# Fp32 pair loads, masks and conversions on GpSimd, and one score buffer given up for highway sums held in PSUM

## The chip, the cores and the metric

The kernel runs on one core of a Trainium2 chip. Times are microseconds (us) on the device for one execution of the whole program. A time that is quoted for a kernel is the median of several runs; comparisons use runs in the fast state only, with a 95% interval. The profile of each kernel is one execution, so the span that it shows is a little shorter than the timed run (134.9 us beside 136.6 us for the kernel before).

Engines: PE is TensorE (matmuls and transposes), DVE is VectorE, ACT is ScalarE, POOL is GpSimd, SP is SyncE, which here only issues DMA transfers.

## The reference

Windowed attention with sink tokens, then a highway layer. There are 4 batches, 8 heads, 768 tokens, head size 64; a token sees the 128 last tokens (itself included) and the first 4 of its batch.

```python
keep = is_sink | in_window          # (rel >= 0) & (rel < 128), or key position < 4
a = softmax(where(keep, q @ k.T / 8, -1e9))
x = (a @ v) -> (3072, 512)          # heads side by side
H = maximum(x @ w_h, 0);  T = sigmoid(x @ w_t + b_t)
out = T * H + (1 - T) * x           # 3072 x 512, fp32
```

Inputs are fp32: q, k and v are 18.9 MB together, the two weight matrices 2.1 MB. The kernel computes in fp16.

## The kernel before

A block is 128 tokens; there are 24 blocks, and c is the place of a block in its batch (0 to 5). For one block the work is: T (transpose q and k), S (scores against this block and the one before, and their exponentials), mask, A (attention times values, "av", and its division by the row sums, "xh"), X (transpose xh), Mt and Mh (the two highway matmuls, "tps" and "hps"), and three elementwise operations on VectorE: dd, ee and the output tokens otok. Blocks with c of 2 or more also need the scores of the four sink tokens ("sk").

The parts that matter here are the loads, the masks, the sink scores and the order of work:

```python
AHEAD = 8
s_ps  = tile_pool(name="ps_s",  bufs=2, PSUM)      # scores: two buffers of two banks
av_ps = tile_pool(name="ps_av", bufs=1, PSUM)
m_ps  = tile_pool(name="ps_m",  bufs=2, PSUM)      # everything else
def load(n):                      # the GpSimd queue converts fp32 -> fp16 on the way
    nc.gpsimd.dma_start(out=qsd, in_=q[b, :, rows, :].transpose([1, 0, 2]))
    nc.gpsimd.dma_start(out=ksd, in_=k[b, :, rows, :].transpose([1, 0, 2]))
# first loads: block 0, 1, q/k of 2, w_t, v of 2, q/k of 3, w_h, then v of 3, blocks 4, 5, ...
def stage_sink(n):
    for t in range(2):
        for hp in range(NHP):
            nc.tensor.matmul(sk[:, t, :], lhsT=ks[:, hp * P:(hp + 1) * P],
                             rhs=qT[:, hp, :], start=(hp == 0), stop=(hp == NHP - 1))
def stage_mask(n):
    for e in es:                  # two halves, 128 x 1024 each, on VectorE
        nc.vector.tensor_tensor(out=ev, in0=ev, in1=m..., op=ALU.mult)
def stage_Mh(n):
    ... hps = xT @ w_h ...
    dd   = max(hps, 0) - xh       # into SBUF, fp16
    ee   = (u + 1) * dd
    otok = 2 * xh + ee            # then stored
# ... (cuts)
for i in range(-2, NB + 1):
    s = i + 1
    if c(i) >= 2 and i % 2 == 0: stage_sink(i)
    stage_S(s)
    stage_A(i)
    stage_T(i + 2)                # the transposes of block i+2 stand BEHIND av of block i
    # loads of block i + 10
    stage_mask(s)
    stage_Mt(i - 1); stage_X(i); stage_Mh(i - 1)
```

TensorE, VectorE and ScalarE carry out their work in the order written, so a piece that waits holds back all that stands behind it on its engine.

The softmax here doesn't subtract the row's maximum and nothing guards it: scores larger than these inputs give would overflow.

## Time and profile before

| | before |
|---|---|
| median of 3 runs | 137.37 us (136.38 to 137.81) |
| span in the profile | 134.9 us |
| block 2 normalised (start of its xh on VectorE) | 26.80 us |
| mean distance of xh, blocks 2 to 19 | 4.70 us |
| mean distance of xh, blocks 19 to 23 | 4.63 us |
| xh of block 23 to the end | 9.75 us |

The last four rows split the span into a start, a steady part and a tail. They are read from the start times of the operation xh, once a block, in the time line of VectorE.

From the page of the kernel before: busy time of each engine; TensorE, VectorE and the DMA engines in 40 slices of the span (a digit is the busy share in tenths); two lines of the queues; and the chain of work that ended last, by engine.

```profile
PE 117.1 (87%) x1312; PEld 73.6 (55%) x1312; DVE 108.5 (80%) x230; ACT 90.4 (67%) x129; POOL 65.7 (49%) x81
...
PE   6657939999999899999999899999998999999720
...
DVE  6153724789988999899898998998989998999590
...
q0 software_dynamic: 75936, 10.49, 116.0%
...
HBM read 20.97 MB, written 6.29 MB: 202 GB/s over the span
...
DVE 33%; PE 32%; ACT 11%; issue 8%; POOL 7%; DMA 6%; DVEq 0%; POOLq 0%
```

TensorE and VectorE are full from slice 8 on, and they share the chain about equally. The busy times by stretch, 25 to 125 us in five stretches, sum to this (100 us in all):

```profile
sum 100.00, PE 96.58 PEld 62.16 DVE 91.97 ACT 77.72 POOL 45.54; mean PE 19.32 PEld 12.43 DVE 18.39 ACT 15.54 POOL 9.11
```

TensorE has 97 of 100 us here and VectorE 92. A converting load is counted by the fp16 bytes that it writes, which are half of what it reads.

VectorE's groups of instructions by line (busy us, mean ns of one | idle time before them and what ended it):

```profile
L247 DVE TENSOR_TENSOR e<-e,mask 128x1024 f16<-128x1024 f16 x32 | 20.5, 682 | 0.0
...
L313 DVE SCALAR_TENSOR_TENSOR dd<-hps,xh 128x512 f16<-128x512 f32 x24 | 16.5, 688 | 4.1 <-PE hps L310 4.1
```

The masks are 20.5 us in these 32 alone, two of 0.68 us a block, and dd waits 4.1 us in all for hps matmuls. The key copy (kT) takes 0.42 us. In the start, TensorE waits for block 3, in the time line of TensorE (start, us, ... , idle time before and what ended it):

```profile
19.49 0.40 PE L180 MATMUL tp<-ident,qsd 128*128 128x128 f16 x4 [1.93 <-DMA qsd<-in_q_dram]
20.32 0.61 PE L182 MATMUL tp<-ident,ksd 128*128 128x128 f16 x4 [0.43 <-DMA ksd<-in_k_dram]
```

### The profile page before, as it was taken

How to read it: one execution, taken by the hardware profiler on the slowest of the kernel's cores; microseconds unless marked ns; L12 is line 12 of the kernel's file. 1: busy time of each engine (PE TensorE's matmuls, PEld its weight loads, DVE VectorE, ACT ScalarE, POOL GpSimd, SP SyncE). 2: the span in 40 equal slices, each digit the busy share in tenths (PEclk: the TensorE clock that was granted, in tenths of full speed). 3: DMA queues.
4: the chain of work that ended last, by engine and by line, in shares of the span. 5: the costliest groups of instructions: out<-in, count | busy, mean ns of one | idle time of the engine just before them, and what ended most of it. 6: DMA issues, size and time to landing. Idle time of an engine off the chain costs nothing.

```text
span 134.9 us, 3378 instructions
## 1 busy us (share of the span) xinstructions
PE 117.1 (87%) x1312; PEld 73.6 (55%) x1312; DVE 108.5 (80%) x230; ACT 90.4 (67%) x129; POOL 65.7 (49%) x81
## 2 busy tenths in 40 slices
PE   6657939999999899999999899999998999999720
PEld 2225625856864466567565557656653685665300
DVE  6153724789988999899898998998989998999590
ACT  3054843779775977977777788779767977973310
POOL 6999747889897789979489370000000000000000
PEclk9999995999999999999999999999999999999996
DMA  0999999999999999999999999122011101101111
GB/s 4 111 123 127 160 188 160 155 181 171 154 198 191 196 151 148 152 195 240 192 194 179 193 194 176 38 80 80 6 78 78 63 19 78 78 5 78 78 78 78
DMA packets 81841, 17.02 MB, mean 126 GB/s; under 512 B 77729, under 2 KB 78753, under 8 KB 81826
## 3 DMA queue, kind: packets, MB, share of 16 engines
q0 software_dynamic: 75936, 10.49, 116.0%
q1 hardware_dynamic: 5890, 6.33, 14.6%
q8 instruction: 10, 0.16, 0.5%
q14 instruction: 5, 0.04, 0.1%
HBM read 20.97 MB, written 6.29 MB: 202 GB/s over the span
## 4 chain that ended last, share of the span: by engine, by line
DVE 33%; PE 32%; ACT 11%; issue 8%; POOL 7%; DMA 6%; DVEq 0%; POOLq 0%
PE hps L310 12%; ACT e L234 7%; DMA ksd<-in_k_dram 6%; DVE ee L316 6%; DVE otok L319 6%; DVE dd L313 6%; DVE e L247 5%; DVE xh L277 5%; PE tps L298 4%; PE xtp L286 4%; PE av L262 3%; DVE kT L186 3%; PE sk L211 3%; ACT qT L185 3%; POOL qsd L83 2%
## 5 line engine op out<-in xcount | busy, mean ns | idle before, releaser
L234 ACT ACTIVATE e<-sps,ebias 128x1024 f16<-128x1024 f32 (+1 forms) x48 | 47.4, 1039 | 11.2 <-PE sps L231 6.0
L298 PE MATMUL tps<-wt_sb,xT 128*128 128x512 f16 x96 | 25.5, 390 | 0.0
L310 PE MATMUL hps<-wh_sb,xT 128*128 128x512 f16 x96 | 24.7, 379 | 0.7
L83 POOL DMA_DIRECT2D qsd<-in_q_dram x24 | 21.6, 900 | 4.7 <-DMA wh_sb<-in_moe_w_h_dram 1.0
L84 POOL DMA_DIRECT2D ksd<-in_k_dram x24 | 21.4, 893 | 3.1 <-PE tp L182 1.3
L262 PEld LDWEIGHTS <-e 128*128 128x128 f16 x352 | 19.8, 98 | 3.2 <-issue 0.4
L301 ACT ACTIVATE u<-tps 128x512 f16<-128x512 f32 x24 | 14.4, 600 | 9.5 <-PE tps L298 9.5
L247 DVE TENSOR_TENSOR e<-e,mask 128x1024 f16<-128x1024 f16 x32 | 20.5, 682 | 0.0
L185 ACT COPY qT<-tp 128x512 f16<-128x512 f16 x24 | 14.0, 585 | 9.6 <-PE tp L182 9.6
L313 DVE SCALAR_TENSOR_TENSOR dd<-hps,xh 128x512 f16<-128x512 f32 x24 | 16.5, 688 | 4.1 <-PE hps L310 4.1
L186 DVE COPY kT<-tp 128x512 f16<-128x512 f16 x24 | 10.1, 423 | 11.7 <-ACT qT L185 11.7
L316 DVE SCALAR_TENSOR_TENSOR ee<-u,dd 128x512 f16<-128x512 f16 x24 | 16.6, 692 | 2.5
L319 DVE SCALAR_TENSOR_TENSOR otok<-xh,ee 128x512 f32<-128x512 f16 x24 | 16.6, 692 | 0.8
L277 DVE TENSOR_TENSOR xh<-av,rec 128x512 f16<-128x512 f32 x24 | 16.6, 691 | 0.8
L231 PE MATMUL sps<-qT,kT 64*128 64x128 f16 x352 | 15.4, 227 | 2.1 <-DVE kT L186 1.1
L231 PEld LDWEIGHTS <-kT 64*128 64x128 f16 x352 | 10.7, 98 | 9.5 <-issue 6.6
L288 ACT COPY xT<-xtp 128x512 f16<-128x512 f16 x24 | 14.0, 583 | 1.1 <-PE xtp L286 0.9
L298 PEld LDWEIGHTS <-xT 128*128 128x128 f16 x96 | 9.6, 100 | 9.1 <-issue 0.8
L310 PEld LDWEIGHTS <-xT 128*128 128x128 f16 x96 | 9.3, 98 | 8.6 <-issue 1.5
L286 PEld LDWEIGHTS <-xh 128*128 128x128 f16 x96 | 6.4, 101 | 13.4 <-DVE xh L277 11.2
L286 PE MATMUL xtp<-ident,xh 128*128 128x128 f16 x96 | 9.9, 228 | 3.8 <-DVE xh L277 3.8
L180 PE MATMUL tp<-ident,qsd 128*128 128x128 f16 x96 | 10.0, 231 | 2.4 <-DMA qsd<-in_q_dram 2.3
(88 smaller groups left out, 152.9 us busy)
## 6 DMA issues: line engine op xcount, KB each, us to landing
out_dram<-otok SPq DMA_DIRECT2D x24, 256.0 KB
qsd<-in_q_dram POOLq DMA_DIRECT2D x24, 128.0 KB, 7.3
ksd<-in_k_dram POOLq DMA_DIRECT2D x24, 128.0 KB, 7.4
wt_sb<-in_moe_w_t_dram POOLq DMA_DIRECT2D x1, 512.0 KB, 8.4
wh_sb<-in_moe_w_h_dram POOLq DMA_DIRECT2D x1, 512.0 KB, 10.1
v_91<-in_v_dram POOLq DMA_DIRECT2D x3, 128.0 KB, 8.0
v_92<-in_v_dram POOLq DMA_DIRECT2D x3, 128.0 KB, 6.1
v_93<-in_v_dram POOLq DMA_DIRECT2D x2, 128.0 KB, 8.0
```

The costliest lines, as they stand in the source:

```text
L83: nc.gpsimd.dma_start(out=qsd, in_=q[b, :, rows, :].transpose([1, 0, 2]))
L231: nc.tensor.matmul(sps[:, hh, o:o + P], lhsT=kk[rows, hp, :], rhs=qT[rows, hp, :], start=True, stop=True)
L234: nc.scalar.activation(out=e.rearrange("p a b c d -> p a (b c d)"), in_=sps[:, :, 0:2 * np_ * P], func=AF.Exp, bias=ebias, scale=SCALE)
L247: nc.vector.tensor_tensor(out=ev, in0=ev, in1=m.unsqueeze(1).to_broadcast([P, 4, np_ * P]), op=ALU.mult)
L262: nc.tensor.matmul(av[:, g, 2 * hl + hh, 0:_AVN], lhsT=es[g][:, hh, hl, pc, :], rhs=vt[:, 65 * h:65 * h + _AVN], start=first, stop=False, ...
L277: nc.vector.tensor_tensor(out=xh, in0=avh[:, :, 0:D], in1=rec.unsqueeze(2).to_broadcast([P, H, D]), op=ALU.mult)
L286: nc.tensor.transpose(xtp[:, j, :], xh[:, 2 * j:2 * j + 2, :], ident)
L298: nc.tensor.matmul(tps, lhsT=xT[:, kc, :], rhs=wt_sb[:, kc, :], start=False, stop=(kc == NOC - 1))
L310: nc.tensor.matmul(hps, lhsT=xT[:, kc, :], rhs=wh_sb[:, kc, :], start=(kc == 0), stop=(kc == NOC - 1))
L313: nc.vector.scalar_tensor_tensor(out=dd, in0=hps, scalar=0.0, in1=xh, op0=ALU.max, op1=ALU.subtract)
L316: nc.vector.scalar_tensor_tensor(out=ee, in0=u, scalar=1.0, in1=dd, op0=ALU.add, op1=ALU.mult)
L319: nc.vector.scalar_tensor_tensor(out=otok, in0=xh, scalar=2.0, in1=ee, op0=ALU.mult, op1=ALU.add)
```

## The change

Its intent: take the masks off VectorE. GpSimd spends its time issuing the converting loads, so these go first. After the first four blocks, q, k and v come as plain fp32 through SyncE's queue, two blocks at once for q and k (512 contiguous bytes rather than 256), and GpSimd converts them to fp16 in SBUF. GpSimd then has time for masks. The second score buffer (two PSUM banks) is given up so that the transposes, the bias, the sinks and the highway sum have banks of their own; the highway sum stays in PSUM through dd and ee, so that each of VectorE's large operations has only one SBUF input. The sink scores are made by narrow matmuls of 32 columns of weights each; the matmuls of their exponentials with the sinks' values (in av) use 64 rows of the array, and the bias row the other 64, so that these two can run side by side.

```diff
-    s_ps = ctx.enter_context(tc.tile_pool(name="ps_s", bufs=2, ...))
+    s_ps = ctx.enter_context(tc.tile_pool(name="ps_s", bufs=1, ...))
+    UB = 2; NFINE = 4; NV = 6
     def load_v(n):
-        nc.gpsimd.dma_start(out=vt[:, :, 0:D], in_=v[...])
+        nc.sync.dma_start(out=t, in_=v[...])                       # fp32
+    def load_unit(u):                                              # q, k of two blocks
+        nc.sync.dma_start(out=staged[name, u]...,
+            in_=src[b, :, t0:t0 + UW, :].rearrange("h (p j) d -> p h (j d)", j=UB))
+    def cast(name, u):  nc.gpsimd.tensor_copy(out=sd16[name, u]..., in_=staged...)
+    def cast_v(n):      nc.gpsimd.tensor_copy(...)
+    # first loads on GpSimd: block 0, 1, w_t, 2, w_h, 3
     def stage_T(n):
+        # tokens 2p+j of a pair lie in partition p: written back with stride two
+        dst = qkT_u[u].rearrange("p a (t j) -> p a t j", j=UB)[:, :, :, j]
     def stage_mask(n):
-        two products with a mask on VectorE
+        nc.gpsimd.affine_select(...)   # twice, 128 x 1024; chunks 0 and 1 partly on VectorE
     def stage_X(n):
-        nc.scalar.copy(out=xT, in_=xtp)
+        nc.vector.tensor_copy(out=xT, in_=xtp)
     def stage_Mh(n):
-        dd, ee in SBUF; otok in the same iteration
+        hps = max(hps, 0) - xh; hps = (u + 1) * hps      # in place, in PSUM
+    def stage_out(n): otok = 2 * xh + hps                # one iteration later
 # order of work
-    s = i + 1:  sink, S(s), A(i), T(i+2), mask, Mt(i-1), X(i), Mh(i-1)
+    s = i + 2
+    i == -2: load_unit(2), v 4, v 5, load_unit(3), v 6, v 7      # SyncE
+    S(s) first half, T(i+4), bias(i-1), A(i), out(i-2), S(s) second half, sink(i+1),
+    Mt(i-1), X(i), mask(s), Mh(i-1)
+    # T: i < 0: block i+3; i == 0: blocks 3 and 4; then block i+4
```

Note two things that are easy to pass over. The transposes now stand ahead of av in the order of TensorE, and they are those of block i+4. And scores of the first block of a pair need the transposes of both, because the pair's tokens are interleaved.

## The prediction

> **What bounds it now.** The span is 134.9 us. In the stretch view from 25 to 125 us, VectorE is busy 92 of 100 us, TensorE 97, ScalarE 78. The chain of waits gives VectorE 33% and TensorE 32%. One block takes about 4.65 us (first AV matmuls of block 2 at 25.3 us, of block 23 about 97 us later, 21 blocks). VectorE's work per block, from the group lines, is 4.6 us: two masks of 0.68, kT 0.42, xh, dd, ee, otok 0.69 each, rec 0.20. So VectorE is full and TensorE is nearly full. DMA is busy in every slice up to 84 us, but nothing waits for it after about 24 us: the loads bound the start only (k of block 3 lands at 20.3 us), not the steady part.
>
> **What the change does, per block.** VectorE loses the masks (kept for chunks 0 and 1, 0.68 each), gains xT (0.42, from ScalarE); kT is written with stride two and may go from 0.42 to 0.69. Sum about 4.1 us. ScalarE falls from about 4.0 to 3.4. TensorE saves the bias matmul (0.22) where it runs beside the sink matmuls, which use the other 64 rows: about 4.0.
> VectorE's remaining large operations have one SBUF input each, the other in PSUM. By the Trainium skill ("SBUF — State Buffer", Who interferes with whom) these do not contend with GpSimd; no trace shows it yet. GpSimd gets 1536 converted and up to 2048 masked elements a block. Its 128-element select took 0.33 us here; taking 0.1 us as fixed (its one-element memset) gives up to 1.8 ns an element. Estimate 3.5 to 5 us a block: below the period if lucky.
>
> **The new wait.** The highway sum has one PSUM bank, held until otok, which runs one iteration later behind kT, rec and xh. So Mh of a block waits for otok of the block before. Loop: Mh (1.02, first start to end) - dd (0.79 to the next start) - ee 0.61 - kT 0.34 to 0.60 - rec 0.23 - xh 0.62 - otok 0.69 - hand-over 0.1 = 4.4 to 4.65 us. That is hardly less than now, though VectorE is busy only 4.1 of it; xT and the remaining masks fit inside the Mh gap. I expect 4.4 for most blocks and about 3.9 for the last four, without transposes: 17 x 0.25 + 4 x 0.75 = 7 us gained.
>
> **The start.** Block 3 is now needed one iteration earlier, wh is loaded ahead of it, and five v loads plus three q/k units run beside the cast loads. Output stores now do not slow the cast loads (150 GB/s alone, up to 261 with them, stretch view), so I expect the delay small: AV of block 2 at about 29 to 30 us, 4 us lost. Tail as now, about 12 us.
>
> **Predicted: 134.5 us (before 137.37), range 127 to 147.** Chances: faster by over 2% 0.44, within 2% 0.26, slower 0.30.
>
> **What would show it.** VectorE at about 85 to 90% in the steady part, idle before dd, released by hps matmuls; hps matmuls waiting for VectorE otok; kT at 0.69 or 0.42; xh, dd, ee still 0.69 while GpSimd is busy; the first otok near 33 us; GpSimd below 90% busy.
>
> **What would make it wrong.** GpSimd selects over 1.9 us make GpSimd the bound (5 us or more a block). VectorE's two-SBUF masks of chunks 0 and 1 block behind a GpSimd instruction, 1 to 2 us eight times. The fp32 loads starve the cast loads at the start, with TensorE idle to 30 us or more: 10 us lost. Or the kernel is faster, if hps is released sooner than the loop says.

## The result

| | before | after |
|---|---|---|
| median of 3 runs | 137.37 us | 156.97 us (156.86 to 157.29) |
| block 2 normalised | 26.80 us | 44.57 us |
| distance, blocks 2 to 19 | 4.70 us | 4.86 us |
| distance, blocks 19 to 23 | 4.63 us | 4.14 us |
| xh of block 23 to the end | 9.75 us | 11.33 us |
| span in the profile | 134.9 us | 155.1 us |

The kernel is slower: the ratio is 1.1447 with a 95% interval of 1.1346 to 1.1549. Ratios here and below are the mean time of one kernel's fast runs over that of the other's fast runs of the same rounds, so they are not quite the ratios of the medians. Executions over 1.5% slower than the fastest of the same kernel are left out of the means.

The four rows of the middle explain the 20.3 us in the span: start +17.8, steady part 17 x 0.17 = +2.9, last four blocks -1.9, tail +1.6. The start is nearly all of it.

From the page of the changed kernel, the same parts, and the row of the granted TensorE clock:

```profile
PE 122.8 (79%) x1280; PEld 69.4 (45%) x1280; DVE 106.4 (69%) x217; ACT 83.1 (54%) x105; POOL 84.2 (54%) x97
...
PE   6424421269999999899999998999999899998820
...
DVE  6031120145487799997779999897799997777761
...
PEclk9999999999999999999999999999999999999997
...
DVE 38%; PE 33%; DMA 14%; POOL 5%; issue 4%; ACT 3%; DVEq 0%; POOLq 0%; ACTq 0%
```

TensorE is busy for only 10 to 60% of each slice up to slice 8 (31 us), and DMA has 14% of the chain where it had 6%. After that TensorE is as full as before, and VectorE is not: the change did relieve VectorE. GpSimd is busy for 54% of the span, so it is not the bound.

The pieces of the chain in the start, in order of time (start us, us, what):

```profile
9.19 7.67 DMA ksd<-in_k_dram
16.86 13.65 DMA k_196<-in_k_dram
...
30.63 1.05 POOL ksd L122
...
31.73 0.61 PE tk L221 x4
```

One load of k, for blocks 4 and 5, takes from 16.86 to 30.51 us; GpSimd converts it, and only then can TensorE transpose block 4. Av of block 0 stands behind these transposes. The k of block 3, whose transposes began at 20.32 us before, is transposed from 28.55 us on.

One block of the steady part, from the same chain:

```profile
70.52 0.94 PE hps L379 x4
...
71.48 0.71 DVE hps L382
...
72.29 0.70 DVE hps L384
72.98 0.64 DVE qkT L227
...
73.84 0.69 DVE xh L349
74.54 0.60 DVE otok L391
...
75.18 1.02 PE hps L379 x4
```

This is the loop that the prediction named: hps of one block, then five VectorE operations and otok, which alone frees the one bank of hps for the next block: 4.66 us around in this block. The groups that answer to those of before, and the new select:

```profile
L227 DVE COPY qkT<-tk 128x512 f16<-128x512 f16 x24 | 16.3, 679 | 22.7 <-PE tk L221 22.7
L311 POOL TENSOR_SCALAR_AFFINE_SELECT e<-e 128x1024 f16<-128x1024 f16 x16 | 17.5, 1091 | 25.2 <-ACT e L290 19.7
...
L382 DVE SCALAR_TENSOR_TENSOR hps<-hps,xh 128x512 f32<-128x512 f32 x24 | 16.7, 696 | 9.7 <-PE hps L379 9.6
```

The key copy costs 0.68 us in the mean rather than 0.42 (0.73 for the pair blocks). The select costs 1.09 us. The operation on hps takes 0.70 us, as dd did, and the idle time before it has grown from 4.1 to 9.7 us, nearly all of it (9.6) ended by hps matmuls.

### The profile page after: what moved, and what is told of

Read it like the earlier page. It is cut to its first block, busy times and chain, and to the rows that moved or that the text cites. A ratio compares the mean times of both kernels' runs of the same rounds, so it can differ in the third digit from the quotient of the medians.

```text
span 155.1 us, 3328 instructions
## 1 busy us (share of the span) xinstructions
PE 122.8 (79%) x1280; PEld 69.4 (45%) x1280; DVE 106.4 (69%) x217; ACT 83.1 (54%) x105; POOL 84.2 (54%) x97
## 3 DMA queue, kind: packets, MB, share of 16 engines
HBM read 20.97 MB, written 6.29 MB: 176 GB/s over the span
## 4 chain that ended last, share of the span: by engine, by line
DVE 38%; PE 33%; DMA 14%; POOL 5%; issue 4%; ACT 3%; DVEq 0%; POOLq 0%; ACTq 0%
PE hps L379 13%; DMA k_196<-in_k_dram 9%; DVE hps L384 8%; DVE hps L382 8%; DVE otok L391 7%; DVE xh L349 7%; DVE qkT L227 5%; PE tps L367 5%; DMA ksd<-in_k_dram 5%; PE sps L288 4%; PE av L339 4%; ACT e L290 3%; DVE e L300 3%; PE sk L266 2%; PE tq L221 1%
## 5 line engine op out<-in xcount | busy, mean ns | idle before, releaser
L227 DVE COPY qkT<-tk 128x512 f16<-128x512 f16 x24 | 16.3, 679 | 22.7 <-PE tk L221 22.7
L311 POOL TENSOR_SCALAR_AFFINE_SELECT e<-e 128x1024 f16<-128x1024 f16 x16 | 17.5, 1091 | 25.2 <-ACT e L290 19.7
L313 POOL TENSOR_SCALAR_AFFINE_SELECT e<-e 128x1024 f16<-128x1024 f16 x20 | 21.8, 1092 | 13.2 <-ACT e L290 13.2
L367 PE MATMUL tps<-wt_sb,xT 128*128 128x512 f16 x96 | 25.3, 387 | 0.0
L232 ACT COPY qkT<-tq 128x512 f16<-128x512 f16 x24 | 17.0, 706 | 15.2 <-PE tq L221 15.2
L382 DVE SCALAR_TENSOR_TENSOR hps<-hps,xh 128x512 f32<-128x512 f32 x24 | 16.7, 696 | 9.7 <-PE hps L379 9.6
L288 PE MATMUL sps<-qkT 64*128 64x128 f16 x352 | 19.6, 232 | 2.8 <-ACT e L290 2.0
L221 PE MATMUL tq<-ident,qsd 128*128 128x128 f16 x96 | 10.8, 243 | 10.5 <-DMA qsd<-in_q_dram 10.5
L384 DVE SCALAR_TENSOR_TENSOR hps<-u,hps 128x512 f32<-128x512 f16 x24 | 16.7, 696 | 2.9 <-DVE hps L382 0.5
L288 PEld LDWEIGHTS <-qkT 64*128 64x128 f16 x352 | 11.1, 99 | 14.6 <-issue 11.7
L391 DVE SCALAR_TENSOR_TENSOR otok<-xh,hps 128x512 f32<-128x512 f16 x24 | 16.3, 678 | 0.1
L221 PE MATMUL tk<-ident,ksd 128*128 128x128 f16 x96 | 10.6, 241 | 6.1 <-DMA ksd<-in_k_dram 3.9
```

Of the source, the lines that this page charges most:

```text
L221: nc.tensor.transpose(tp[:, jj, :], sd[:, j, 2 * jj:2 * jj + 2, :], ident)
L227: nc.vector.tensor_copy(out=dst[:, NHP:2 * NHP], in_=tps[1])
L288: nc.tensor.matmul(sps[:, hh, o:o + P], lhsT=kk[rows, hp, :], rhs=qT[rows, hp, :], start=True, stop=True)
L313: nc.gpsimd.affine_select(out=ev[:, :, 1, :], in_=ev[:, :, 1, :], pattern=[[0, H], [1, P]], **keep_cur)
L367: nc.tensor.matmul(tps, lhsT=xT[:, kc, :], rhs=wt_sb[:, kc, :], start=False, stop=(kc == NOC - 1), skip_group_check=True)
L382: nc.vector.scalar_tensor_tensor(out=hps, in0=hps, scalar=0.0, in1=xh, op0=ALU.max, op1=ALU.subtract)
```

## The experiments

Eighteen kernels ran. All gave correct results. "xh(2)" is the start of xh of block 2, "period" the mean distance of xh of blocks 2 to 19, both from the profiled run of that kernel. Ratios are to the kernel before. The medians count every run; the ratio of e10 (1.125) counts its two slow runs too (155.16 and 155.29 us); its two fast ones, 152.65 and 152.88 us, are 1.116 of the fast runs before. For e13 to e15 the whole 95% interval lies above 1.05; for e16 and e17 it reaches across a gain of 2%. In e5 the late start falls on block 3, which is why no period is given.

| run | what | median us | ratio | xh(2) us | period us |
|---|---|---|---|---|---|
| before | | 137.37 | | 26.8 | 4.70 |
| after | | 156.97 | 1.145 | 44.6 | 4.86 |
| e1 | first v loads a little later | 154.79 | 1.132 | 42.8 | 4.85 |
| e2 | six blocks converted in flight, fp32 later | 148.45 | 1.085 | 37.2 | 4.82 |
| e3 | e2, weights later, transposes later | 153.20 | 1.112 | 40.4 | 4.85 |
| e4 | highway sum freed at once | 154.62 | 1.130 | 44.6 | 4.71 |
| e5 | before + the first fp32 loads, unused | 150.22 | 1.099 | 30.7 | - |
| e6 | after + all loads as before | 154.72 | 1.131 | 35.9 | 5.19 |
| e7 | fp32 loads by single rows | 156.91 | 1.146 | 45.6 | 4.75 |
| e8 | before + half of the masks on GpSimd | 163.32 | 1.196 | 44.1 | 5.26 |
| e9 | eight blocks converted in flight | 154.10 | 1.124 | 36.3 | 5.26 |
| e10 | e9 + sum freed | 154.02 | 1.125 | 34.6 | 5.14 |
| e11 | e4 + bias over 128 rows | 157.00 | 1.146 | - | - |
| e12 | before + narrow sinks | 135.70 | 0.991 | 27.5 | 4.63 |
| e13 | after + av ahead of transposes | 156.75 | 1.144 | 44.1 | 4.90 |
| e14 | e9 repaired + av ahead | 147.79 | 1.078 | 31.2 | 5.08 |
| e15 | e14 + sum freed | 147.29 | 1.068 | 32.3 | 4.91 |
| e16 | e12 + highway later, weights later | 134.08 | 0.983 | 21.8 | 4.70 |
| e17 | e16 + key copy of odd blocks on ScalarE | 134.85 | 0.974 | 21.2 | 4.75 |
| e18 | e14 + conversions earlier | 149.10 | 1.093 | 31.1 | 5.13 |

### The start: which loads, and in front of what

My first theory was that the fp32 loads take memory traffic away from the converting loads that the first blocks need. The rival was that only a part of them, or the new order of work, does it.

**e1** puts the first v loads behind a small operation that waits for the constants:

```diff
+        if n < NFINE + 6:
+            nc.vector.memset(t[0:1, 0, 0:1], 0.0)
         nc.sync.dma_start(out=t, in_=v[...])
```

> Changed kernel with one edit: the first six fp32 loads of v wait for the constants (about 10 us) instead of going out at 1 us. Theory 'every packet of the fp32 queue that is there before block 3 has landed takes a turn from the cast queue': blocks 0 and 1 land about 2 us earlier, but the same v packets then compete later, so k of block 3 still lands at 27 to 29 us and the time falls by 2 us at most. Rival 'the five early v loads are what delays the start': k of block 3 at about 23 us, time 5 us lower.

The held-back loads moved packets from 17.0 us on rather than 1.9, and block 2 came 1.8 us earlier. So it is not the early place of the v loads that makes the late start; their bytes still compete later.

**e2** lets the converting queue load blocks 0 to 5 and holds all fp32 loads until the keys of block 3 are transposed:

```diff
-    NFINE = 2 * UB
+    NFINE = 3 * UB
-    i == -2: load_unit(...), load_v(...)
+    i == 0, behind the transposes of block 3: load_unit(...), load_v(...)
```

> Changed kernel, but blocks 4 and 5 also come through the cast queue and no fp32 load goes out before k of block 3 has been copied. Theory 'the fp32 queue takes the cast queue's turns at the start': k of block 3 lands at about 23 us instead of 28.5, xh of block 2 at 33 to 35 us instead of 44.6, time 146 to 149. Rival 'the later weights order or the extra look-ahead is the cause': k of block 3 lands before 25 us but xh of block 2 stays after 40 us, time above 152.

This gives 7.3 us back in the start (37.2 us, expected 33 to 35), and 8.5 us in all: the largest gain in time by loads alone, but far from 17.8.

**e3** also puts the weights behind block 3, and each transpose as late as the pairs allow.

> As the run before, and the two weights behind block 3, and block 4 transposed only with block 5, as late as the pairs allow. If order and look-ahead cost what is left of the start, xh of block 2 comes at 27 to 29 us as in the kernel before (26.8), time 140 to 143; the steady part stays at 4.86 us a block, so it must remain slower than the kernel before by its 17 x 0.17 us and more.

Theory missed (27 to 29 us and 140 to 143 us were expected). Block 0 is normalised at 18.2 us, but block 1 only at 33.4: the held-back fp32 loads went out at 17.7 us and block 4 of the converting queue, which av of block 1 now had to wait for, could be transposed only at 27.5 (q) and 30.3 us (k). The starvation moved and was not removed.

**e5** turns the question round: the kernel before, with the same first fp32 loads into tiles that nobody reads.

```diff
+    for n in range(5): extra_v(n)           # fp32, 0.26 MB each, at once
+    if i == -2:
+        for x in range(6): extra_unit(x)    # fp32, 0.5 MB each
```

> The kernel before with one thing added: the fp32 loads of the changed kernel's start (five of v at once, six half-megabyte ones of q and k after the first constants), into tiles that nobody reads. Theory 'these loads take the cast queue's turns': k of block 3 lands at 26 to 29 us instead of 20.3, xh of block 2 moves from 26.8 to 32 to 35 us, time 143 to 146. Rival 'the start is late for the changed kernel's look-ahead and order of the weights, not for the fp32 loads': less than 2 us.

It loses 13.4 us, more than the 6 to 9 expected, and most of it later than at block 2 (30.7 us rather than 26.8). The transposes of k of block 4 in its time line of TensorE:

```profile
36.49 0.61 PE L196 MATMUL tp<-ident,ksd 128*128 128x128 f16 x4 [2.66 <-DMA ksd<-in_k_dram]
```

Before, they stood at 26.57 us and waited for no load; here they start at 36.49, and those of q at 33.43 (26.35 before), each after a wait of some 3 us for its load. Xh of block 3 comes at 43.8 rather than 31.8 us, that of block 4 at 50.5 rather than 36.3, and the distances of later blocks are the same as before. So the loads alone, with no other part of the change, make a late start of 12 us at block 3 and 14 us at block 4. (They are 5 x 0.26 + 6 x 0.52 = 4.4 MB that no one reads.)

How that happens can be counted. I summed the packet records of the trace up to the moment at which xh of block 2 starts, with the converting queue's bytes doubled, because it reads twice what it writes. Before, 6.8 MB had been read by 26.8 us; after, 11.9 MB by 44.6 us. Counted from 2 us on, that is 0.275 and 0.280 MB a us. In every run here the figure at this point lies between 0.24 and 0.29. So the queues share one supply, whose mean rate hardly depends on who asks. (It is a mean: in stretches of 2 us of the changed kernel the rate goes from 0.22 to 0.40, highest where the weights with their long rows are read. Whether memory or the DMA engines set it, no run here shows.) The 5.1 MB more, at 0.28 MB a us, are 18.2 us: the late start of 17.8. By itself this agreement shows no cause, because a supply that is never idle has moved more bytes at any later moment, whatever the delay: e8, with no fp32 loads at all, had read 11.5 MB when its xh of block 2 started, at 44.1 us. That the loads delay the start is shown by e5 and by the square below. The shared supply agrees with the Trainium skill, "DMA: Bandwidth & Descriptors", section Issuing engines are not separate DMA queues: transfers run on the same 16 DMA engines and interleave, whoever issues them.

The records also show how the two share. Between 24 and 28 us of the changed kernel they count about 332 records with data a us for each of the two queues: one for one. This fits what the same page says under Queues, rings and completion order (the engines take turns, packet by packet), but does not show the length of a turn: a packet of that page typically holds 9 to 17 descriptors, and what part of one a record of the trace is, is not shown. A record of the fp32 pair loads holds 512 bytes, one of the converting loads reads 256. So in this stretch the loads that were not yet needed got two thirds of the bytes.

What the count leaves open is why 11.9 MB had to land first. **e9** loads eight blocks by the converting queue, the later ones as fp32 by single rows, and holds the fp32 loads until the keys of block 6 are transposed. (The gate covered only the first of the two loads of a pair, so two loads, 0.52 MB, still went out at once; the same holds for e7, e10, e14, e15 and e18.)

> The changed kernel with blocks 0 to 7 loaded by the converting queue (as before the change) and every fp32 load held back until the keys of block 6 are transposed; fp32 loads of q and k by single rows, so that a block's transposes can wait for it alone. Theory (the fp32 loads take the memory traffic of the converting loads, and that alone makes the late start): the normalise operation of block 2 comes at 26 to 29 us rather than at 44.6, and nothing is lost later: about 4.75 us a block, time 138 to 141 us. Rival (the late start comes from needing block 3 an iteration earlier, or from the new order of work): it stays at 35 us or later, time 147 or more. If the starvation only moves again, a gap of several us shows at block 8 or 9, where the fp32 loads begin.

Theory missed: 36.3 us rather than 26 to 29, although only these 0.52 MB of fp32 data had landed by then (its profiled run was 1.8% above its fastest run, which is not enough to explain 7 us). So the sharing is not all of it. I then read the order of TensorE: transposes of block i+3 or i+4 stand ahead of av of block i. Before, av of block 2 needed blocks 0 to 3. After, it needs blocks up to 6.

**e13** changes this order alone, in the first iterations:

```diff
-    T(...), bias(i-1), A(i)
+    bias(i-1), A(i), T(...)          # for i <= 3
-    i == 0: blocks 3, 4;  then i+4
+    i == 0: block 3;  i == 1: blocks 4, 5;  then i+4
```

> The changed kernel with the order of the first iterations alone changed: AV of block i goes ahead of the transposes that stand in the same iteration, and the transposes of blocks 4 and 5 come one iteration later. All loads as after the change. Theory (what must have landed before AV of a block is set by TensorE's order): block 0 is normalised at 20 to 22 us rather than 33.4, block 1 at about 30, block 2 at 35 to 38 rather than 44.6; time 147 to 151 us. Rival (the sharing of memory between the two kinds of loads is all of it): block 2 stays within 2 us of 44.6 and the time within 2 us of 157.

Block 0 was normalised at 23.5 us rather than 33.4, as expected, but block 2 at 44.1: the theory in this form missed, and the rival in this test was right. The keys of block 3 still came late, at 29.14 us, and from there on TensorE waited for only 1.9 us until av of block 2. The edit had left the scores of block 4, and with them the transposes of blocks 4 and 5, which are one pair, ahead of av of block 2. So this run tests the order for block 0 and hardly for block 2.

**e14** does both: e9 with av ahead of the transposes up to iteration 4, and the weights in the order of before. Two further gates and earlier conversions came with it; the 0.52 MB escaped here too, so one of the repairs that the expectation names did not take.

> The run with eight blocks by the converting queue, with four repairs: AV of block i ahead of the transposes up to iteration 4, weights in the order of before, three fp32 loads that had escaped the gate held back too, and the conversions one iteration earlier. Theory: both parts of the late start are gone, block 2 is normalised at 26.5 to 29 us, then 4.75 us a block; time 137 to 141 us. Rival (something else in the change holds the start): 33 us or later. A gap of some us at block 8 or 9, where the held-back fp32 loads begin, would put it at 142 to 146.

Block 2 was normalised at 31.2 us, between the theory (26.5 to 29) and its rival (33 or later). The k of block 3 is transposed at 20.42 us, the same time as before the change (20.32).

The four kernels form a square. Start of xh of block 2:

| | transposes ahead of av | av ahead of transposes |
|---|---|---|
| fp32 loads early | 44.6 (after) | 44.1 (e13) |
| fp32 loads held back | 36.3 (e9) | 31.2 (e14) |

The loads are worth 8.3 us with the new order and 12.9 with the old one; the order is worth 0.5 us while the loads are early and 5.1 once they are not. Together they explain 13.4 of the 17.8 us. The corner of e9 also has another order of the weights, both lower corners have eight blocks in the converting queue, and their single-row loads free the scores of block 4 from the transposes of block 5; so the split between the two is not exact.

The other 4.4 us can be read from the time lines of TensorE, from the keys of block 3 to av of block 2. Before, the keys are transposed at 20.32 us (line above), and av follows at

```profile
25.32 0.22 PE L262 MATMUL av<-v_92,e 128*128 128x112 f16 x1
```

In the changed kernel:

```profile
28.55 0.61 PE L221 MATMUL tk<-ident,ksd 128*128 128x128 f16 x4 [2.52 <-DMA ksd<-in_k_dram]
...
31.73 0.61 PE L221 MATMUL tk<-ident,ksd 128*128 128x128 f16 x4 [2.14 <-POOL ksd L122]
...
42.99 0.40 PE L329 MATMUL av<-vs_135,es 64*128 64x260 f16 x2
```

and in e14:

```profile
20.42 0.61 PE L227 MATMUL tk<-ident,ksd 128*128 128x128 f16 x4 [0.23 <-DMA ksd<-in_k_dram]
...
29.63 0.39 PE L335 MATMUL av<-vs,es 64*128 64x260 f16 x2
```

From keys to av it takes 5.0 us before, 14.4 in the changed kernel (2.1 of them the wait for the keys of block 4) and 9.2 in e14, where the keys are on time. So the 4.4 us left in e14 lie behind the keys of block 3, in TensorE's own work (its order, and the slow matmuls named below), and not in the escaped loads: av of block 1, the transposes of block 4 and scores of blocks 3 and 4 now stand in between. The late start of 17.8 us is likewise 8.2 us until the keys of block 3 and some 9.4 after them.

TensorE's matmuls were also slow in the start: four transposes took 0.61 us up to about 36 us in the changed kernel, and 0.39 from 41 us on; before, they took 0.39 from 26 us on. The clock row of e4, whose block 2 is normalised at the same moment, shows why: the granted clock was 0.5 from 8 to 39 us. (The trace of the changed kernel has no clock record before 40.6 us, so the 9s in its row up to there say nothing.) So a late start also makes the work behind it slower; how many of the 9.4 us that is was not separated.

The time of e14 fell by only 9 us, because it lost some 5 us again at blocks 14 and 15. **e18** tried to mend this by moving the conversions to the start of an iteration.

> The run with eight blocks by the converting queue and AV ahead of the transposes, with the conversions back at the start of an iteration from iteration 4 on, as the change has them. Theory: block 2 normalised at 31 us, no gap at block 14, 4.75 to 4.85 us a block, time 141 to 144 us: that is 13 to 15 of the 20 us lost, and what stays is the rest of the start (4 us), the steady loop (3 us) and the tail. Rival (the gap comes back elsewhere because of the late fp32 loads): 146 to 149.

The start is the same (31.1 us), and the gap stayed: the distances into blocks 14 and 15 are 9.2 and 6.1 us, so 149.1 us rather than the 141 to 144 expected. SyncE's issues in this stretch, from its time line:

```profile
79.16 2.55 SPq L102 DMA_DIRECT2D q<-in_q_dram  x2
81.75 2.90 SPq L102 DMA_DIRECT2D k<-in_k_dram  x2
84.74 5.02 SPq L252 DMA_DIRECT2D vs<-v  x8
```

The loads by single rows are two issues each, and they took 1.2 to 1.5 us apiece rather than 0.4, which is what one takes in the changed kernel at the same place. The eight small copies of the sinks of batch 2 stand behind them and took until 89.8 us, and av of block 14 waited for the last of them. It is the same mistake as in the start, on a smaller scale: loads that are needed later stood in front of those needed now. Without the 5.8 us of these two distances the span of e18 would be 141.2 us (147.0 - 5.8, an estimate).

**e6** is the changed kernel with all loads by the converting queue, as before, and masks still on GpSimd.

> The changed kernel with the loads of the kernel before: every block of q, k and v through the converting queue, weights in the old order, no conversion on GpSimd, transposes copied without the stride of two. Start theory: xh of block 2 at 27 to 30 us instead of 44.6. Loop theory: kT takes 0.42 instead of 0.73 us, so the loop hps - dd - ee - kT - rec - xh - otok falls below TensorE's own work of about 4.7 us a block; period 4.6 to 4.75. Time 135 to 141. If the loads are not the cause of the start, above 148. If GpSimd (2.7 us of load issue and 2.2 of selects a block) is now the bound, the period is above 4.85.

It took 154.72 us, rather than the 135 to 141 expected, and block 2 came at 35.9 us though no fp32 loads were there. With three issues of 0.9 to 1.1 us and two selects of 1.1 to 1.3 us a block, GpSimd became the bound: 7.1 us a block until about 50 us. So the masks cannot simply move to GpSimd while it issues the loads; the change needed other loads.

**e8** asks the same of the kernel before: only half of the masks of chunks 2 to 5 go to GpSimd.

> The kernel before with one part of the change alone: in chunks 2 to 5 GpSimd masks the first half of the heads (two selects of 512 elements), VectorE the second. VectorE loses 0.68 us in 16 of 24 blocks. If VectorE and GpSimd do not hold each other up, the period falls from 4.70 to about 4.5 (TensorE) and the time to 132 to 135. If VectorE's operations with two inputs in SBUF (mask, ee, otok) are held behind GpSimd's selects or load issues, they take 0.3 to 0.6 us longer now and then, and the time is 136 or more.

It took 163.32 us. GpSimd works in order: selects wait behind load issues for buffers, and load issues behind selects for scores. After the loads had ended (about 106 us), its periods were 4.55 and 4.99 us, exactly those of the kernel before: with half of the masks gone, VectorE had less to do and nothing became faster. That is the first sign that VectorE was not the only bound.

### The steady part: the one sum, and TensorE

The theory of the prediction was a loop through the one bank of hps. **e4** breaks it: hps matmuls go ahead of the transposes of xh, and otok follows ee directly.

```diff
-    stage_out(i - 2)                          # otok one iteration later
     stage_Mt(i - 1)
+    stage_Mh_pe(i - 1); stage_dd(i - 1)       # hps matmuls and dd
     stage_X(i); stage_mask(s)
-    stage_Mh(i - 1)
+    stage_ee(i - 1); stage_out(i - 1)
```

> Changed kernel, start untouched; the highway sum's bank is given back one iteration earlier: otok follows ee at once, and the hps matmuls stand before the xtp transposes. Theory 'the loop hps - dd - ee - kT - rec - xh - otok - hps sets the period': the steady period (xh of block 2 to block 19) falls from 4.86 to about 4.5 us, where TensorE's own work is the bound, VectorE waits little for hps, time about 150. Rival 'GpSimd slows VectorE, or TensorE is the bound already': period stays at 4.8 to 4.9.

The start was the same to a hundredth (44.57), the period 4.71 us rather than 4.86, the time 154.62: a smaller gain than the 4.5 us and 150 us expected, but not the rival's 4.8 to 4.9 either. The loop is gone from the chain, and TensorE alone is in its place:

```profile
68.92 0.86 PE hps L377 x4
69.78 0.22 PE xtp L358 x4
...
73.48 0.86 PE hps L377 x4
```

From one hps to the next the chain has nothing but TensorE's pieces, without a gap: 4.56 us in a block without sink scores. I added up TensorE's pieces from the starts in its time line. Before the change: scores 0.55, av 0.81 and its sinks 0.22, transposes 0.44, bias 0.22, Mt 0.86, xtp 0.22, hps 0.86, sum 4.2 us, and 4.7 with sink scores (0.54). After: the scores come as two pieces of 0.33, av 0.90, the transposes 0.55, bias and sinks in av 0.32, Mt 0.97, xtp 0.22, hps 0.94, sum 4.6, and 4.9 with sink scores (0.33). So the change put 0.2 to 0.4 us a block on TensorE, which was nearly full: before, the sums lie some 0.3 us below the distances (4.55 and 4.99); in e4 they are the distance. Eight score matmuls take 0.33 us alone, and 16 take 0.55 together, so each separate piece costs about 0.11 us more (2 x 0.33 - 0.55). Each of these pieces is a change between 64-row and whole-array matmuls. The Trainium skill, "TensorEngine Tiling (Array Packing)", section Key Properties, says that a change of tiling mode drains TensorE; it gives no cost. The 0.11 us fit that, but no run here separates a drain from another fixed cost.

**e7** loads q and k as fp32 by single rows of 256 bytes, so the copies need no stride.

> The changed kernel with the fp32 loads of q and k by single rows (256 bytes a packet, two loads for each) instead of pairs of rows, so that the transposes are copied without a stride. Loop theory: kT 0.42 instead of 0.73 us, period from 4.86 to 4.6 to 4.75 (TensorE bound). Start: as many bytes in twice the packets, each taking a turn, so the start is later by 0 to 4 us. Time 151 to 157. If the stride does not matter, period 4.86.

The key copy went from 0.68 us back to 0.42, as in the kernel before; the period fell by 0.12 us and the start grew by 1.1 (here, too, 0.52 MB of fp32 loads went out at 1.9 us, past the gate), so the time was the same as after the change (156.91). The stride was a real cost in the loop: the Trainium skill, "VectorE: DVE Perf Modes", section What auto-detection actually checks, allows the faster 16-bit mode for steps of one only, and the trace agrees (0.42 us with step one, 0.73 with step two).

**e10** and **e15** add the freed sum to e9 and e14.

> The run before, and the highway sum freed in the same iteration (output token right after the gate product, hps matmuls ahead of the transposes of the normalised block). Theory: both losses are taken back but the split scores and 64-row sinks still cost TensorE about 0.3 us a block, so the period is 4.60 to 4.70 us and the time 135 to 138 us, the same as before the change within 2%. Rival (only the start and the one sum mattered): 4.4 us a block, 131 to 133 us.

> The run before with the highway sum freed in the same iteration. Theory: start of 27 to 29 us, 4.65 to 4.75 us a block bounded by TensorE's own work; time 135 to 139 us, within 2% of before the change: the idea's gain on VectorE (about 0.5 us a block) is not cashed because TensorE is the next bound. Rival (TensorE has slack): 4.4 us a block, 131 to 133 us.

The fast runs of e10 (152.65 and 152.88 us) are 0.7% below those of e9, and e15 was 1% faster than e14 at most: the times 135 to 139 and 131 to 133 us were both missed, because of the gap at block 14 and because many blocks took 5.0 us. In e15 the distances into blocks 6, 7 and 8 were 4.26, 4.27 and 4.33 us, but they follow one of 6.41, so some of that may be catching up; single distances are shorter still (3.7 us in e15, 4.14 in e4). I did not find a version that keeps such a pace.

**e11** takes the bias matmul back to all 128 rows, with the sum freed as in e4.

> The kernel with the sum freed, and the bias matmul over all 128 rows again (the sinks stay in 64 rows). Theory (a change between whole-array and 64-row matmuls costs about as much as the overlap saves): the period stays within 0.05 us of 4.71 us, time within 1% of 154.6 us. Rival (the bias row beside the sinks saves its 0.22 us, as the change intends): two thirds of the blocks have sinks, so the period rises by 0.12 to 0.2 us, time 157 to 158 us.

157.00 us beside 154.62 (ratios 1.146 and 1.130): my theory missed and the rival was right. The bias beside the sinks saves some 2.3 us in all. That part of the change pays. The profiled run of e11 fell in a very slow state (288 us, the hps matmuls at 842 ns in the mean rather than 378), so its trace is not used.

### What helps the kernel before

**e12** changes only the sink scores of the kernel before: each matmul writes its own 32 rows.

```diff
-    nc.tensor.matmul(sk[:, t, :], lhsT=ks[:, hp * P:(hp + 1) * P],
-                     rhs=qT[:, hp, :], start=(hp == 0), stop=(hp == NHP - 1))
+    nc.tensor.matmul(sk[32 * hp:32 * hp + 32, t, :], lhsT=ks[:, hp * 160:hp * 160 + 32],
+                     rhs=qT[:, hp, :], start=True, stop=True, skip_group_check=True)
```

> The kernel before with one line changed: each of the four sink-score matmuls of a block writes its own 32 output rows from 32 columns of weights, rather than all four adding up over 128 columns. Theory (TensorE bounds the blocks with sink scores, 4.99 us against 4.55, and the 8 sink matmuls of 0.54 us become cheaper when four of them can run in different column groups): the sink phase takes 0.15 to 0.33 us, those 8 blocks take 4.6 to 4.8, 1.5 to 3 us less in all, time 134 to 136 us. Rival (matmuls in different column groups run one after the other): the phase stays at 0.5 us and the time within 0.5 us of before.

The time lines of TensorE, first of the kernel before:

```profile
80.48 0.61 PE L211 MATMUL sk<-qT,ks_154 128*128 128x128 f16 x8
81.02 0.62 PE L231 MATMUL sps<-qT,kT 64*128 64x128 f16 x16
```

and of e12:

```profile
80.52 0.30 PE L211 MATMUL sk<-qT,ks 128*32 128x128 f16 x8
80.75 0.62 PE L232 MATMUL sps<-qT,kT 64*128 64x128 f16 x16
```

From its start to that of the scores, the piece went from 0.54 to 0.23 us, and the blocks with sink scores from 4.99 to 4.77. The Trainium skill says that different tiles of the array can work in parallel ("TensorEngine Tiling (Array Packing)", Key Properties); this agrees. The time is 135.70 us, ratio 0.991 (0.986 to 0.996): a small gain. The time lies in the range expected (134 to 136); the gain over the runs before of its own rounds (136.91) is 1.2 us, a little less than the 1.5 to 3 expected.

**e16** applies the lesson of the start to the kernel before: the weights are loaded behind the first five blocks, and the highway matmuls stand two iterations behind the attention rather than one.

```diff
-    load order: 0, 1, 2, w_t, 3, w_h, 4, ...      highway of block i-1
+    load order: 0, 1, 2, 3, 4, w_t, w_h, 5, ...   highway of block i-2
```

> The kernel before with narrow sink matmuls, the highway matmuls of block i two iterations behind its attention rather than one, and the weights loaded behind the first five blocks. Theory (the start waits for bytes that are not needed yet): block 2 is normalised at 20 to 23 us rather than 26.8, TensorE works in that gap, and the time falls by 1.5 to 3 us below the run with narrow sinks (135.7): 132.5 to 134.5. Rival (the same bytes are only waited for later, at the first highway matmuls): 135 to 136.5.

Block 2 is normalised at 21.8 us rather than 26.8, as expected. The tail grows from 9.75 to 11.9 us, because one more block of highway work is left at the end. The time is 134.08 us, ratio 0.983 (0.977 to 0.990): the fastest median here, ahead of both kernels. The gain is near 2% and the record's verdict is "unclear".

**e17** then takes the key copy of odd blocks off VectorE.

> The run with the highway two iterations behind, with the key copy of odd blocks made by ScalarE (0.58 us) rather than VectorE (0.42). Theory (VectorE, 4.6 us of work a block, bounds the blocks of 4.55; ScalarE has 3.9 us): the mean period falls by 0.1 to 0.2 us and the time from 134.1 to 130.5 to 132.5. Rival (the chain from transposes over the score exponentials on ScalarE to the masks is the bound too): a key copy queued on ScalarE delays the exponentials, and the time stays at 133.5 to 136.

VectorE's busy time in the stretch from 25 to 120 us fell from 88.3 to 84.8 us, and the steady distances stayed at 4.4 to 4.8: no gain from it that I can show. Three of its six runs were slow, so its median (134.85) and its ratio (0.974, fast runs) point different ways. Its own theory (130.5 to 132.5 us) missed. Together with e8 this says that in this kernel relief for VectorE alone buys no gain clear of noise.

## Why the prediction was wrong

**The step that failed** is the start: "Output stores now do not slow the cast loads ... so I expect the delay small: AV of block 2 at about 29 to 30 us, 4 us lost." Measured: 17.8 us (xh of block 2 at 44.57 rather than 26.80; its av at 43 us rather than 25.3). With 4 us in place of 17.8 the time would have been about 143 us, inside the predicted range. Two readings in it were wrong.

- I took 150 GB/s of the converting loads for their use of memory, and 261 GB/s with output stores for proof of spare room. But these loads are counted by the fp16 bytes that they write: the page itself has 10.49 MB for the queue and 20.97 MB read. Memory was already being read at about 0.28 MB a us. And the stores did slow the loads: in the kernel before, from 66 to 68 us, without stores, the loads read 0.30 MB a us; from 60 to 62 us, while stores wrote 0.17, they read 0.15. Reads and writes together stayed at 0.30 to 0.32, and the rise to 261 GB/s came from half of the reads not being counted. There was no spare room, and the fp32 loads took two thirds of the bytes while both queues were full (24 to 28 us).
- I saw that block 3 "is now needed one iteration earlier", and gave it no size. In TensorE's order, av of block 2 had moved behind the transposes of block 6. The square of runs above gives this order 5.1 us once the loads are out of the way (with the order of the weights in it), and the 4.4 us that e14 leaves are TensorE's own work behind the keys of block 3 too, more of it and part of it at a low clock.

The prediction had named the case among what would make it wrong ("The fp32 loads starve the cast loads at the start ... 10 us lost"). It was the main case, and larger.

**Mis-sized terms of the steady part.**

- The loop through hps was named rightly, with the right links: hps waits for otok (2.6 us in 9 waits in the changed kernel), dd waits for hps (9.6 us in 17 waits). It was sized at 4.4 to 4.65 us, and most distances are 4.72 to 4.88, because the step from the key copy is 0.64 to 0.71 rather than "0.34 to 0.60", and dd and ee take 0.80 and 0.70 to the next start.
- TensorE was sized at "about 4.0" us. Its pieces sum to 4.6, and 4.9 with sink scores: the scores in two pieces, dearer transposes and av. This is the term that would have kept the change from paying even with a perfect start: e4 removes the loop and gains 0.15 us a block.
- GpSimd was sized at 3.5 to 5 us a block, the feared bound. Its select is 1.09 us and its conversion 1.04, about 3.3 us a block; it was busy for 54% of the span.
- The last four blocks were expected at 3.9 us and took 4.14. The tail was expected "as now" and grew by 1.6 us.

**What was right.** The key copy with stride two costs 0.73. VectorE's operations with one SBUF input were not slowed by GpSimd, as the prediction drew from the Trainium skill ("SBUF — State Buffer", Who interferes with whom): xh took 0.692 us (0.691 before) and ee 0.696 (0.692 before). And the masks with two SBUF inputs do contend, as it feared: of the four of chunk 1, the three that overlapped a select of GpSimd took 1.35 us each and the one that overlapped nothing took 0.69, where a product of that size takes 0.68 in the kernel before.

## What to carry to other kernels

Count what must have landed before the first useful result: list, in each engine's order, what stands in front of it, add the bytes, and divide by the rate at which all queues together are served (here 0.24 to 0.29 MB a us in the mean of the start). Each step of look-ahead puts more work in front of that first result. Loads for later blocks on a second queue are not free; hold them until the first ones have landed, and remember that a converting load is counted by what it writes, so that room which the counted rate shows may not be there. And before moving work off a full engine, ask which other engine is as full: here TensorE nearly was, and what the move added there cost more than VectorE gained.

## What the Trainium skill lacked or had wrong

- "DMA: Bandwidth & Descriptors", Queues, rings and completion order, says that engines take turns by packet. It lacks what follows for bytes: two full queues with records of 256 and 512 bytes were served about 332 records a us each, so the bytes were split one to two.
- The same page lacks that a profile counts a converting load by its written bytes (10.49 MB for 20.97 MB read here), so that its rate looks like half of the memory traffic.
- The same page lacks what an issue on SyncE costs while its queue is backed up: 3 to 3.9 us for each of the first half-megabyte loads, and 1.2 to 1.5 us in e18, where it is 0.35 to 0.45 us otherwise.
- "TensorEngine Tiling (Array Packing)", Key Properties, gives no cost for a change of tiling mode. Eight 64-row score matmuls took 0.33 us as a piece of their own and 16 took 0.55 in one piece: about 0.11 us for each further piece.
- "GPSIMD Engine Reference" has no cost for an affine select that I found: 1.09 us for 128 x 1024 fp16, 0.33 us for 128 x 128.
- "TensorE: Matmul & The Clock Gate", Part 1, warns that records of the clock can be unreliable, and the runs agree: in the changed kernel four transposes took 0.61 rather than 0.39 us up to about 36 us, while its row of the granted clock shows 9 there, because its first record comes at 40.6 us. In e4, with the same start, the row shows 0.5 from 8 to 39 us. Mean granted clocks (0.994 and 0.895 in these two) cannot be compared then.
- The same part mentions a clock stuck low for 50 us and more. The profiled run of e11 shows matmuls slow for a whole execution: 288 us rather than 157, hps matmuls at 842 ns in the mean rather than 378, with no clock record at all (the mean is listed as 1.0). One run of the kernel before was as slow (279.92 us).
